# Zero products in fp32 instead of fp16, and two FFN blocks in two column pieces each

## The chip, the core and the metric

The kernel runs on one core of a Trainium2 chip. The metric is the time of one execution on the device in microseconds; the number for a kernel is the median of several runs. Profiled executions come with a span, from the first to the last instruction of the program, which is a little shorter than the device time of the same execution. TensorE (PE) multiplies, its weight loads (PEld) overlap with the products; VectorE (DVE), ScalarE (ACT) and GpSimd (POOL) do elementwise work; SyncE (SP) issues most of the transfers.

## The reference

A retention layer with a decaying state, step by step over 768 positions, for 4 batches and 8 heads of 64, then a feed-forward part with a product of two branches and no nonlinearity. All inputs and the output are fp32.

```python
gamma = 1.0 - 2.0 ** (-5.0 - np.arange(H))
for t in range(S):
    state = gamma * state + k[:, :, t] (x) v[:, :, t]       # 64 x 64 per head
    y[:, :, t] = q[:, :, t] @ state / sqrt(D)
x = y as 3072 rows of 512
out = ((x @ w1) * (x @ w2)) @ w3 @ w_out                    # 512 -> 1024 -> 512
```

## The kernel before

The 3072 rows are cut into twelve tiles of T = 256 positions, three to a batch, n = 0 to 11; the tile that the words call the seventh has n = 6. The recurrence is computed in chunks. For each tile there are `scores` (k against q inside a chunk, line 406), `kv` (the chunk's own state, line 454), `inter` (the carried state against q, line 521, in two halves with `fence` between them) and `av` (masked scores against v, line 548). All of these are 64x64 products that use one quarter of the array each; `QUARTERS` (line 377) names the four quarters in the order in which every group of four goes through them. The text calls them the quarter groups. `x_out` scales the result into `XT`, in fp16.

The feed-forward part multiplies w3 and w_out with each other first (`turn_w3`, `turned_w3`, `w3_mm`, `w3_out`; lines 278 to 307), as soon as their rows arrive, and keeps the product in `W3O`. Then each tile needs four pairs of blocks: `two_blocks` (line 578) makes 2 x 128 columns of x @ w1 ("a") or x @ w2 ("b") from eight products of 256 columns in one bank of PSUM; `a_evac` copies "a" out on ScalarE, `b_evac` multiplies it by "b" on VectorE. `blk` (line 704) calls `two_blocks`, and `evac` the two evacuations. `o_unit` (line 636) multiplies the result with `W3O`; it already has a parameter `pieces`, which the calls for n = 5 set to 2.

The order of everything is written out by hand, from line 713 to the end: each engine runs its own instructions in that order, with semaphores between engines. In the steady part one round is: the quarter groups of two neighbouring tiles, `o_unit` and `o_copy` of an earlier tile, then the eight blocks of a tile with their evacuations. The loads are issued by `fetch` and `load` on SyncE.

At the start TensorE has little to do, since the weights are still arriving. `warm(m, tag, w)` (line 688) then issues m products of zeros into a bank of PSUM that nobody reads: 128 x 128 zeros against w columns of zeros, from the tile `zeros` (line 135), which is 512 columns of fp16 and is cleared as 256 columns of fp32. Each call takes the bank `tag` anew. `warm(8)` stands ahead of the first transposes of w3 (`turn_w3(4, "S0")`), the calls with "F2" between the transposes of rows 4, 1 and 2.

Of the kernel before, what the change touches and what calls it, by code (L numbers as in the profile page):

```python
# [9 lines left out]
FP = mybir.dt.float32  # L10
# [10 lines left out]
def kernel(  # L21
# [11 lines left out]
    nc = tc.nc  # L33
    B, H, S, D = q.shape
    T = 256
# [35 lines left out]
    def bank(tag, shape, dtype=FP):  # L71
        return psum.tile(shape, dtype, tag=tag, name="ps" + tag)
# [47 lines left out]
    def fetch(names, via=nc.sync):  # L120
        for x in names.split():
            kind, i = x[:-1], int(x[-1])
            if kind == "r":
                w3_st[i] = load_rows(moe_w3, i, via)
            elif kind == "wo":
                wo_st[i] = load_wo(i, via)
            elif kind in ("w1", "w2"):
                w_st[kind, i] = load_rows({"w1": moe_w1, "w2": moe_w2}[kind], i, via)
            else:
                load(kind, i)  # L130
# [4 lines left out]
    zeros = const.tile([128, 512], HP, name="zeros")  # L135
# [14 lines left out]
    def need(*x):  # L150
        assert done.issuperset(x)

    def numbers():
        done.add("numbers")

        nc.gpsimd.iota(key_i[:, :, :], pattern=[[1, 2], [0, H]], base=1 - 128, channel_multiplier=2)
        nc.gpsimd.iota(
            col_i[:, :, :].rearrange("p g (j u) -> p g j u", j=8), pattern=[[128, 2], [1, 8], [8, 16]],
            base=1 - 128, channel_multiplier=0,
        )  # L160
        for h in range(H):
            p = h // 2
            c = place(p, h % 2) * 64
            nc.gpsimd.memset(LGH[:, h : h + 1], -math.log(gam[h]))
            nc.gpsimd.memset(LGP[c : c + 64, p : p + 1], math.log(gam[h]))

    def keeps():
        done.add("keeps")
        nc.gpsimd.memset(keep[:, :, :], 1.0)
        for g in range(2):  # L170
            rows = slice(g * 64, g * 64 + 64)
            for t in range(2):
                nc.gpsimd.affine_select(
                    out=keep[rows, t, :], in_=keep[rows, t, :], compare_op=GE, fill=0.0,
                    base=-t, pattern=[[1, 8], [8, 16]], channel_multiplier=-2,
                )
# [28 lines left out]
    W1 = [wpool.tile([128, DFF], HP, name=f"w1_{i}") for i in range(4)]  # L205
    W2 = [wpool.tile([128, DFF], HP, name=f"w2_{i}") for i in range(4)]
# [35 lines left out]
    def step_decays():  # L242
        done.add("decays")
        for h in range(H):
            r, p = (h % 2) * 64, h // 2
            nc.gpsimd.memset(GS[r : r + 64, p, :], gam[h] ** T)
# [22 lines left out]
    def cast_wo(i, eng):  # L269
        done.add(("wo", i))  # L270
        split(eng, WO[i][:, :, :].rearrange("p a n -> p (a n)"), wo_st[i][:, :])

    def cast_w3(f, eng):
        w3h[f] = att.tile([128, 1024], HP, tag="kq"[len(w3h_tags) % 2] + "16", name="w3h", bufs=3)
        w3h_tags.append(f)
        split(eng, w3h[f][:, :], w3_st[f][:, :])

    def turn_w3(f, tag):
        need("identity")
        src, ps = w3h.pop(f), bank(tag, [128, 1024], HP)  # L280
        for g in range(8):
            c0 = g // 2 * 256 + g % 2
            nc.tensor.transpose(ps[:, g * 128 : (g + 1) * 128], src[:, c0 : c0 + 255 : 2], ident16[:, :])  # L283
        w3p[f] = ps

    def turned_w3(f, eng):
        w3t[f] = fsb.tile([128, 1024], HP, tag="pa", name="w3t", bufs=8)
        split(eng, w3t[f][:, :], w3p.pop(f)[:, :])
# [23 lines left out]
    q16, k16, v16, qT, kT, qP, am, XT, TS, KB, X = {}, {}, {}, {}, {}, {}, {}, {}, {}, {}, {}  # L312
# [262 lines left out]

    HT, pa, ht_n = {}, {}, {}

    def two_blocks(W, n, u, tag):
        need(*[(w, d, c) for w in ("w1", "w2") for d in range(4) for c in (0, 512)])
        assert x_n[n] == 2  # L580
        ps = bank(tag, [128, 2, T])
        for i in range(2):
            f = 2 * u + i
            for d in range(4):
                nc.tensor.matmul(  # L585
                    ps[:, i, :], lhsT=W[d][:, f * 128 : (f + 1) * 128], rhs=XT[n][:, d, :],
                    start=(i == 0 and d == 0), stop=(i == 1 and d == 3),
                )
        return ps

    def a_evac(n, u, ps, eng="s"):
# [9 lines left out]
    def a_unit(n, u, tag, eng="s"):  # L601
        a_evac(n, u, two_blocks(W1, n, u, tag), eng)

    def b_unit(n, u, tag):
        b_evac(n, u, two_blocks(W2, n, u, tag))
# [54 lines left out]
    def o_copy(n, tb, c0=0, c1=512, eng="s"):  # L660
        dst, src = o_tile(n, tb)[:, c0:c1], o_ps.pop((n, tb, c0, c1))[:, :]
        if eng == "s":
            nc.scalar.activation(dst, src, AF.Copy, scale=final_scale)  # L663
        else:
            nc.vector.tensor_scalar_mul(dst, src, final_scale)
        o_n[n] = o_n.get(n, 0) + (c1 - c0)
        o_n[n, tb] = o_n.get((n, tb), 0) + (c1 - c0)
# [17 lines left out]
            o_copy(n, tb, *c)  # L685
            o_store(n, tb, *c)

    def warm(m, tag="X1", w=512):
        ps = bank(tag, [128, 512])
        for _ in range(m):  # L690
            nc.tensor.matmul(ps[:, 0:w], lhsT=zeros[:, 0:128], rhs=zeros[:, 0:w], start=True, stop=True)

    def cast_w(W, st, d, eng, c0=0, c1=DFF):
        done.update((st, d, c) for c in range(c0, c1, 512))
# [6 lines left out]
    ab = {}  # L701
    cuts = ((0, 320), (320, 512))

    def blk(w, n, u, tag):
        ab[w, n, u] = two_blocks(W1 if w == "a" else W2, n, u, tag)

    def evac(w, n, u, eng="s"):
        if w == "a":
            a_evac(n, u, ab.pop((w, n, u)), eng)
        else:  # L710
            b_evac(n, u, ab.pop((w, n, u)))
# [33 lines left out]
    fetch("q3")  # L745
    identity()
    fetch("q4")
    warm(8)
    numbers()
    arguments()  # L750
    tables(4)
# [2 lines left out]
    tables(2)  # L754
    cast_w3(4, "v")
    turn_w3(4, "S0")
    warm(3, "F2")
    turned_w3(4, "v")
    step_decays()
    warm(2, "F2")  # L760
    cast_wo(0, "s")
    cast_w3(1, "v")
    keeps()
    warm(1, "F2")
    cast_w3(2, "gs")
    warm(1, "F2")
    turn_w3(1, "S1")
    tables(0)
    fetch("v3")
    turned_w3(1, "sv")  # L770
    warm(3, "F2")
    cast_wo(1, "g")
    turn_w3(2, "X0")
    w3_mm(1, 0, "S1", first=True)
# [206 lines left out]
    x_out(2, 1)  # L981
    dma_turn("q", 4)
    blk("a", 2, 0, "F0")
    cast_v(4, "g")
    evac("a", 2, 0)
    blk("b", 2, 0, "F1")
    kv(3, ("X0", "K"))
    turned("q", 3, "v")
    state(3, 1)
    fetch("k5")  # L990
    fetch("v5")
    blk("b", 2, 1, "F0")
    state(3, 2)
    blk("a", 2, 1, "F2")
# [180 lines left out]
    o_copy(5, 0)  # L1175
    o_unit(5, 1, ("F0",), pieces=2)
    o_copy(5, 1)
    blk("a", 6, 0, "F2")
    evac("a", 6, 0)
    blk("b", 6, 0, "F0")  # L1180
    evac("b", 6, 0)
    blk("a", 6, 1, "F1")
    evac("a", 6, 1)
# [245 lines left out]
```

## Time and profile before

| | us |
|---|---|
| median of 3 runs | 181.31 |
| lowest and highest run | 181.07, 181.83 |
| the profiled execution, device time | 181.6 |
| its span | 179.9 |
| ScalarE, VectorE, GpSimd busy | 66.1, 103.0, 63.6 |

How to read it. A row of a timeline has the start and the time that the row covers in us, then engine, line, operation, output and inputs, shape, and the number of instructions that were merged into it; in square brackets stands idle time of the engine before it and what ended it. A matmul's duration in a row goes from its start to the end of its way through the array, and the next one starts well before that, so the rate of a row of products is seen from start to start: the time that the row covers, less one duration, over the number of products less one. In a row of a table by stretches come the stretch, its length, then busy us and number of instructions of PE, PEld, DVE, ACT and POOL, TensorE's granted clock, the busy share of the DMA engines and GB/s. In the chain of waits a line gives start, length and what the end waited for through that time; "SPq" is SyncE's queue. A group of the list of costly lines gives busy us in all and mean ns of one behind the first bar, idle time before it behind the second. A view of one tile or line gives the least, median and largest duration in ns and the first and last start. The row of an instruction queue (q8) gives packets, MB and the share of the DMA engines.

### The profile page before, as it was taken

To read this page: it belongs to the slowest core of one execution; us is meant where nothing else is said; L and a number is where in the kernel's file an instruction comes from. 1 tells how busy PE (TensorE), PEld (TensorE's weight loads), DVE (VectorE), ACT (ScalarE), POOL (GpSimd) and SP (SyncE) were. 2 spreads that over 40 slices of the span, in tenths; PEclk is the share of its full clock that TensorE was granted. 3 is DMA by queue.
4 is the path that set the end of the run, shared out by engine and by line. 5 is a ranking of instruction groups with operands and counts; after the bars stand their busy time and mean duration, and the time that the engine had idled before them with its cause. 6 is when DMAs were issued, how large, how long until landed. Compare 5 with 4: busy or idle time off the path is not lost.

```text
span 179.9 us, 6072 instructions
## 1 busy us (share of the span) xinstructions
PE 173.4 (96%) x2642; PEld 125.7 (70%) x2642; DVE 103.0 (57%) x177; ACT 66.1 (37%) x118; POOL 63.6 (35%) x93
## 2 busy tenths in 40 slices
PE   7989899999999999999999999999999999999993
PEld 2445456688956785885867898768688587786872
DVE  2342789883946487547366384474764946734330
ACT  5436537681238332323314314223222131232422
POOL 7753076446232742724445055250453200000000
PEclk9999999999999999999999999999999999999999
DMA  5999999999899899999999999999999552150303
GB/s 206 409 418 360 357 325 389 408 282 226 181 244 236 204 179 221 202 204 238 178 241 228 237 284 178 212 240 232 271 211 263 170 166 71 70 166 5 117 0 117
DMA packets 80025, 40.22 MB, mean 224 GB/s; under 512 B 59392, under 2 KB 73984, under 8 KB 80000
## 3 DMA queue, kind: packets, MB, share of 16 engines
q1 hardware_dynamic: 79856, 39.33, 88.6%
q8 instruction: 20, 0.33, 0.8%
q10 hardware_dynamic: 144, 0.52, 0.8%
q14 instruction: 5, 0.04, 0.1%
HBM read 29.36 MB, written 6.29 MB: 198 GB/s over the span
## 4 chain that ended last, share of the span: by engine, by line
PE 72%; DMA 15%; SPq 5%; POOL 3%; ACT 2%; DVE 1%; issue 1%; POOLq 0%; DVEq 0%
PE psF L585 38%; PE psF L643 20%; DMA st<-in_v_dram 8%; DMA st<-in_q_dram 4%; DMA st<-in_moe_w_dram 4%; SPq L112 3%; PE psX L521 2%; POOL v L69 2%; PE psX L548 2%; PE psS L406 1%; PE psK L299 1%; PE psF L299 1%; ACT pa L61 1%; SPq L89 1%; PE psF L621 1%; PE psX L621 1%
## 5 line engine op out<-in xcount | busy, mean ns | idle before, releaser
L585 PE MATMUL psF<-xt,w 128*128 128x256 f16 x640 | 71.9, 273 | 0.0
L585 PEld LDWEIGHTS <-w 128*128 128x128 f16 x640 | 62.4, 98 | 9.2
L69 DVE TENSOR_TENSOR ht<-pa,psF 128x512 f16<-128x512 f32 x43 | 29.4, 687 | 38.9 <-PE psF L585 38.8
L61 ACT COPY pa<-psF 128x512 f32<-128x512 f32 x43 | 25.2, 585 | 51.2 <-PE psF L585 45.6
L643 PE MATMUL psF<-w3o,ht 128*128 128x512 f16 (+3 forms) x200 | 38.4, 346 | 0.0
L643 PEld LDWEIGHTS <-ht 128*128 128x128 f16 x224 | 20.7, 98 | 17.5
L69 POOL TENSOR_TENSOR v<-st,VN 128x1024 f16<-128x1024 f32 x10 | 19.0, 1902 | 37.2 <-DMA st<-in_v_dram 18.5
L663 ACT ACTIVATE osb<-psF 128x512 f32<-128x512 f32 (+2 forms) x18 | 9.9, 550 | 31.0 <-PE psF L643 31.0
L566 DVE TENSOR_TENSOR xt<-psX,YN 128x512 f16<-128x512 f32 x19 | 12.8, 724 | 5.7 <-PE psX L548 5.7
L426 DVE TENSOR_TENSOR am<-psS,keep 128x512 f16<-128x512 f32 x19 | 12.5, 681 | 2.6 <-PE psF L406 2.6
L621 PEld LDWEIGHTS <-w 128*128 128x128 f16 x128 | 12.1, 98 | 2.4 <-issue 0.5
L61 POOL CAST q<-st 128x1024 f16<-128x1024 f32 x10 | 10.4, 1039 | 7.2 <-DMA st<-in_q_dram 4.3
L61 POOL CAST k<-st 128x1024 f16<-128x1024 f32 x9 | 9.3, 1036 | 6.2 <-PE psX L548 3.1
L299 PEld LDWEIGHTS <-w3t 128*128 128x128 f16 x64 | 5.8, 98 | 6.4 <-issue 0.7
L621 PE MATMUL psF<-xt,w 128*128 128x256 f16 x56 | 9.7, 272 | 0.0
L69 POOL TENSOR_TENSOR t<-s,GS 128x256 f16<-128x256 f32 x8 | 5.8, 727 | 11.0 <-DVE s L69 11.0
L521 PE MATMUL psX<-qT,t 64*64 64x64 f16 (+1 forms) x296 | 7.6, 199 | 0.0
L69 POOL TENSOR_TENSOR v<-st,VS 128x1024 f16<-128x1024 f32 x2 | 3.9, 1932 | 8.9 <-DMA st<-in_v_dram 8.9
L521 PEld LDWEIGHTS <-t 64*64 64x64 f16 x320 | 4.9, 106 | 3.0 <-issue 2.5
L69 DVE TENSOR_TENSOR t<-psK,t 128x256 f16<-128x256 f32 x15 | 6.2, 415 | 0.4
L283 PEld LDWEIGHTS <-w3h 128*128 128x128 f16 x64 | 4.2, 101 | 2.9 <-DVE w3h L61 1.4
L621 PE MATMUL psX<-xt,w 128*128 128x256 f16 x32 | 6.1, 273 | 0.1
(127 smaller groups left out, 192.4 us busy)
## 6 DMA issues: line engine op xcount, KB each, us to landing
st<-in_moe_w_dram SPq DMA_DIRECT2D x15, 512.0 KB, 8.7
st<-in_k_dram SPq DMA_DIRECT2D x20, 256.0 KB, 5.7
st<-in_q_dram SPq DMA_DIRECT2D x10, 512.0 KB, 6.1
st<-in_v_dram SPq DMA_DIRECT2D x20, 256.0 KB, 4.6
out_dram<-osb SPq DMA_DIRECT2D x9, 512.0 KB, 5.4
st<-in_moe_w_out_dram SPq DMA_DIRECT2D x4, 512.0 KB, 9.8
st<-in_k_dram SPq DMA_DIRECT2D x2, 512.0 KB, 6.5
st<-in_q_dram SPq DMA_DIRECT2D x8, 128.0 KB, 6.5
```

Of the source, the lines that this page charges most:

```text
L61: {"v": nc.vector.tensor_copy, "g": nc.gpsimd.tensor_copy, "s": nc.scalar.copy}[eng](dst, src)
L69: (nc.vector if eng == "v" else nc.gpsimd).tensor_tensor(dst, a, b, op)
L112: via.dma_start(t[:, :].rearrange("p (t n) -> p t n", t=2), moe_w_out[i * 256 : (i + 1) * 256, :].rearrange("(p t) n -> p t n", t=2),)
L283: nc.tensor.transpose(ps[:, g * 128 : (g + 1) * 128], src[:, c0 : c0 + 255 : 2], ident16[:, :])
L299: nc.tensor.matmul(acc[f][:, :], lhsT=w3t[f][:, g * 128 : (g + 1) * 128], rhs=WO[i][:, r, :], start=(first and r == 0), stop=(last and r = ...
L426: nc.vector.tensor_tensor(t[:, :, :, :].rearrange("p a s i -> p (a s) i"), ps[:, :, :, :].rearrange("p a s i -> p (a s) i"), keep64[:, :]. ...
L521: nc.tensor.matmul(dst, lhsT=TS[n, c][half(r), a, :], rhs=rhs, start=((g, o) not in begun), stop=False, skip_group_check=True,)
L566: nc.vector.tensor_tensor(XT[n][:, :, :].rearrange("p a (s x) -> p (a s) x", s=2)[:, :, g * 64 : (g + 1) * 64].rearrange("p k (i t) -> p k ...
L585: nc.tensor.matmul(ps[:, i, :], lhsT=W[d][:, f * 128 : (f + 1) * 128], rhs=XT[n][:, d, :], start=(i == 0 and d == 0), stop=(i == 1 and d = ...
L621: nc.tensor.matmul(rows_ps[w, n, uh][j // 2][:, j % 2, :], lhsT=W[d][:, f * 128 : (f + 1) * 128], rhs=XT[n][:, d, :], start=(first and j % ...
L643: nc.tensor.matmul(ps[:, x : x + w], lhsT=HT[n][:, f, tb * 128 : (tb + 1) * 128], rhs=W3O[f][:, c0 + x : c0 + x + w], start=(f == 0 and x ...
L663: nc.scalar.activation(dst, src, AF.Copy, scale=final_scale)
```

## The change

`warm` reads the zeros as fp32: the same memory as 256 columns instead of 512, the weights as 128 x 128 of fp32. Its default is now 256 columns, and the calls are written anew: four products for the first eight, then 256 columns for each two and 128 for each odd one of the rest. A call has one width, so an odd number takes two calls. That makes eleven zero products instead of eighteen. `two_blocks` and `blk` get a parameter `pieces`; with 2, each product of 256 columns is made as two of 128 with the same weights, each with a load of its own. The first two blocks of n = 6 are called so: 32 products instead of 16. What is computed stays the same.

```diff
--- before.py
+++ after.py
@@ -575,17 +575,19 @@
 
     HT, pa, ht_n = {}, {}, {}
 
-    def two_blocks(W, n, u, tag):
+    def two_blocks(W, n, u, tag, pieces=1):
         need(*[(w, d, c) for w in ("w1", "w2") for d in range(4) for c in (0, 512)])
         assert x_n[n] == 2
         ps = bank(tag, [128, 2, T])
         for i in range(2):
             f = 2 * u + i
             for d in range(4):
-                nc.tensor.matmul(
-                    ps[:, i, :], lhsT=W[d][:, f * 128 : (f + 1) * 128], rhs=XT[n][:, d, :],
-                    start=(i == 0 and d == 0), stop=(i == 1 and d == 3),
-                )
+                for x in range(0, T, T // pieces):
+                    nc.tensor.matmul(
+                        ps[:, i, x : x + T // pieces], lhsT=W[d][:, f * 128 : (f + 1) * 128],
+                        rhs=XT[n][:, d, x : x + T // pieces], start=(i == 0 and d == 0 and x == 0),
+                        stop=(i == 1 and d == 3), skip_group_check=pieces > 1,
+                    )
         return ps
 
     def a_evac(n, u, ps, eng="s"):
@@ -685,10 +687,10 @@
             o_copy(n, tb, *c)
             o_store(n, tb, *c)
 
-    def warm(m, tag="X1", w=512):
-        ps = bank(tag, [128, 512])
+    def warm(m, tag="X1", w=256):
+        ps, z = bank(tag, [128, 512]), zeros[:, :].bitcast(FP)
         for _ in range(m):
-            nc.tensor.matmul(ps[:, 0:w], lhsT=zeros[:, 0:128], rhs=zeros[:, 0:w], start=True, stop=True)
+            nc.tensor.matmul(ps[:, 0:w], lhsT=z[:, 0:128], rhs=z[:, 0:w], start=True, stop=True)
 
     def cast_w(W, st, d, eng, c0=0, c1=DFF):
         done.update((st, d, c) for c in range(c0, c1, 512))
@@ -701,8 +703,8 @@
     ab = {}
     cuts = ((0, 320), (320, 512))
 
-    def blk(w, n, u, tag):
-        ab[w, n, u] = two_blocks(W1 if w == "a" else W2, n, u, tag)
+    def blk(w, n, u, tag, pieces=1):
+        ab[w, n, u] = two_blocks(W1 if w == "a" else W2, n, u, tag, pieces)
 
     def evac(w, n, u, eng="s"):
         if w == "a":
@@ -745,7 +747,7 @@
     fetch("q3")
     identity()
     fetch("q4")
-    warm(8)
+    warm(4)
     numbers()
     arguments()
     tables(4)
@@ -754,21 +756,23 @@
     tables(2)
     cast_w3(4, "v")
     turn_w3(4, "S0")
-    warm(3, "F2")
+    warm(1, "F2")
+    warm(1, "F2", w=128)
     turned_w3(4, "v")
     step_decays()
-    warm(2, "F2")
+    warm(1, "F2")
     cast_wo(0, "s")
     cast_w3(1, "v")
     keeps()
-    warm(1, "F2")
+    warm(1, "F2", w=128)
     cast_w3(2, "gs")
-    warm(1, "F2")
+    warm(1, "F2", w=128)
     turn_w3(1, "S1")
     tables(0)
     fetch("v3")
     turned_w3(1, "sv")
-    warm(3, "F2")
+    warm(1, "F2")
+    warm(1, "F2", w=128)
     cast_wo(1, "g")
     turn_w3(2, "X0")
     w3_mm(1, 0, "S1", first=True)
@@ -1175,9 +1179,9 @@
     o_copy(5, 0)
     o_unit(5, 1, ("F0",), pieces=2)
     o_copy(5, 1)
-    blk("a", 6, 0, "F2")
+    blk("a", 6, 0, "F2", pieces=2)
     evac("a", 6, 0)
-    blk("b", 6, 0, "F0")
+    blk("b", 6, 0, "F0", pieces=2)
     evac("b", 6, 0)
     blk("a", 6, 1, "F1")
     evac("a", 6, 1)
```

## The prediction

> **What bounds the kernel now.** I read the page first: busy time by engine, then the chain that ended last, then the costliest groups.
>
> ```profile
> span 179.9 us, 6072 instructions
> PE 173.4 (96%) x2642; PEld 125.7 (70%) x2642; DVE 103.0 (57%) x177; ACT 66.1 (37%) x118; POOL 63.6 (35%) x93
> ...
> PE 72%; DMA 15%; SPq 5%; POOL 3%; ACT 2%; DVE 1%; issue 1%; POOLq 0%; DVEq 0%
> ```
>
> TensorE is busy for 96% of the span and holds 72% of the chain. The 15% of DMA is not spread evenly; the chain in order of time, between 8 and 24 us, and the timeline of the first 23 us show where TensorE has room.
>
> ```profile
> 8.18 4.31 SPq L112
> ...
> 14.66 7.06 DMA st<-in_q_dram
> ...
> 21.84 0.70 DVE q L61
> ...
> 22.59 0.62 PE psX L370 x8
> ```
>
> ```profile
> 1.26 3.59 PE L691 MATMUL psX<-zeros 128*128 128x512 f16 x8 [1.26 <-DVE zeros L136]
> ...
> 4.77 0.66 PEld L283 LDWEIGHTS <-w3h 128*128 128x128 f16 x8 [0.83 <-DVE w3h L61]
> ...
> 5.44 2.32 PE L691 MATMUL psF<-zeros 128*128 128x512 f16 x7
> ...
> 7.60 0.45 PEld L283 LDWEIGHTS <-w3h 128*128 128x128 f16 x8 [0.54 <-DVE w3h L61]
> 7.61 0.62 PE L283 MATMUL psS<-ident,w3h 128*128 128x128 f16 x8
> ...
> 8.06 0.81 PE L691 MATMUL psF<-zeros 128*128 128x512 f16 x3
> ...
> 8.95 0.45 PEld L283 LDWEIGHTS <-w3h 128*128 128x128 f16 x8 [0.58 <-POOL w3h L61]
> ...
> 9.12 0.56 ACT L61 COPY w3t<-psS 128x512 f16<-128x512 f16 x1
> ...
> 10.06 0.68 DVE L61 COPY w3t<-psX 128x1024 f16<-128x1024 f16 x1
> ...
> 10.20 1.02 PE L299 MATMUL psS<-wo,w3t 128*128 128x512 f16 x4 [0.62 <-DVE w3t L61]
> ...
> 13.15 0.59 PE L299 MATMUL psS<-wo,w3t 128*128 128x512 f16 x2 [0.19 <-POOL wo L61]
> ...
> 22.59 0.62 PE L370 MATMUL psX<-perm,q 128*128 128x128 f16 x8 [0.59 <-DVE q L61]
> ```
>
> The reader is to see two things. The zero products of line 691 all lie before 9 us, between transposes that wait for casts of weights still arriving. And until 22.59 us the chain runs through SyncE's queue and the landing of the first q; TensorE stands idle before 10.20, 13.15 and 22.59 us for 0.62 + 0.19 + 0.59 = 1.40 us. Later there is one more wait for a cast of v, of 0.33 us; from then to the last store TensorE is continuously busy, so what happens there counts in full.
>
> ```profile
> 61.60 0.19 PE L454 MATMUL psX<-v,k 64*64 64x64 f16 x1 [0.33 <-POOL v L69]
> ```
>
> The other place that the change touches is this steady part. Between two rows of FFN blocks lies a burst of 64x64 products, the quarter groups: some 120 products in 1.2 us. I compared the bursts of the seventh and the tenth tile (inter of n = 6 and n = 9), which issue the same products in the same order; first by stretches, then the end of each in the timeline.
>
> ```profile
> 103.00:104.17 1.17, 1.17 (x122) 1.13 (x121) 0.69 (x1) 0.15 (x1) 0.35 (x1) 1.00 1.22 217
> 138.23:139.57 1.34, 1.34 (x121) 1.26 (x120) 0.69 (x1) 0.15 (x1) 1.34 (x1) 1.00 0.92 180
> ...
> 114.75:115.91 1.16, 1.16 (x121) 1.12 (x120) 0.69 (x1) 0.15 (x1) 0.28 (x1) 1.00 1.11 221
> 150.12:151.28 1.16, 1.16 (x121) 1.12 (x121) 0.69 (x1) 0.15 (x1) 0.00 (x0) 1.00 0.02 7
> ```
>
> ```profile
> 102.80 0.27 PE L585 MATMUL psF<-xt,w 128*128 128x256 f16 x1
> 103.00 0.28 PE L521 MATMUL psX<-qT,t 64*64 64x64 f16 x10
> ...
> 103.68 0.29 PE L521 MATMUL psX<-qT,t 64*64 64x64 f16 x11
> ...
> 103.80 0.44 PE L548 MATMUL psX<-am,v 64*64 64x64 f16 x31
> 104.17 0.39 PE L643 MATMUL psF<-w3o,ht 128*128 128x256 f16 x2
> ```
>
> ```profile
> 138.91 0.41 PE L521 MATMUL psX<-qT,t 64*64 64x64 f16 x12
> 139.15 0.49 PE L548 MATMUL psX<-am,v 64*64 64x64 f16 x32
> 139.57 0.39 PE L643 MATMUL psF<-w3o,ht 128*128 128x512 f16 x1
> ```
>
> The tenth tile's burst is 0.17 us longer. 0.12 of it lies in the second half of inter (0.41 against 0.29) and 0.05 in av behind it, and no semaphore is named there. Other bursts repeat to 0.01 us (1.16 and 1.16 for n = 7 and n = 10).
>
> **The change part by part.**
>
> *Zero products, cold.* Eight of 512 columns become four of 256. In the old ones a start follows a start by (3.59 - 0.63) / 7 = 0.42 us with 0.63 the duration of one; the later ones by (0.81 - 0.38) / 2 = 0.216 us.
>
> ```profile
> L691 PE MATMUL psF<-zeros x10: 376/379/379, 5.4 to 8.5; 128*128 128x512 f16 x10
> L691 PE MATMUL psX<-zeros x8: 606/631/631, 1.3 to 4.2; 128*128 128x512 f16 x8
> ```
>
> No fp32 product is in this trace. From below, its 256 columns could take what 256 fp16 columns take, half of 0.42 us; from above I let it take twice the pair that it replaces, 1.7 us. I take the pair, 0.85 us, because the edit exchanges them two for one all through (512 for 256, and a single one for 128 columns), and the rows in between give no better price. Then the four end at 4.65 us as before, ahead of the cast that releases the transposes at 4.77. Were they shorter, TensorE would only idle until then; and should the spacing of 0.216 then come later than it does now, the next seven at 0.42 would add 1.5 us, which the cover of the next step and the 1.40 us of idle time hide.
> The Trainium skill ("FP8 and Floating Point Precision", section "TensorE Precision Notes") says "True FP32: 4 passes through PE array": 4 x 256 columns are the 1024 of the pair, so by it this term is nothing too; no run here shows it yet.
>
> *Zero products, later.* Seven behind the first transposes and three behind the second become two groups of the same worth, 7 and 3 halves of a fp32 product. But each call takes the bank anew and waits for the call before it. In the row of 5.44 us three such waits stand: 2.16 us to the next start at 7.60, less 7 x 0.216, is 0.65, or 0.215 each. The new list makes five calls instead of four behind the first transposes, and two instead of one behind the second: 0.215 us more each. So the transposes of 7.61 start at 7.82, those of 8.96 at 7.82 + 0.45 + 0.65 + 0.215 = 9.13. What covers it: ScalarE begins the first copy at 9.12, when those transposes (now done by 8.5) have long ended; VectorE begins the second at 10.06, and they end by 9.75. Cost 0. Without this cover it would be 0.43 us at 10.20, and behind that the 0.19 + 0.59 us of waits for POOL and for q still take it.
> A rule that speaks against the change: the Trainium skill ("TensorE: Matmul & The Clock Gate", section "Weight-path perf modes — Fast Weight Load (FWL) and DoubleRow") grants the fast weight load to types other than FP32 only. If each of four passes then waited for a load of 128 columns at the P / 1.2 of the same page (section "LDWEIGHTS (loading the stationary operand)"), 107 ns, a 128-column product would cost 0.43 us, an estimate from that page, and the four of them 0.85 us more; the idle times above would still hide that.
>
> *The two blocks in pieces.* 16 products of 256 columns become 32 of 128, each with its own weight load. They lie in the part that counts.
>
> ```profile
> L585 PE MATMUL psF<-xt,w 128*128 128x256 f16 x640 | 71.9, 273 | 0.0
> L585 PEld LDWEIGHTS <-w 128*128 128x128 f16 x640 | 62.4, 98 | 9.2
> ```
>
> ```profile
> L283 PE MATMUL psF<-ident,w3h x24: 219/219/219, 15.8 to 27.6; 128*128 128x128 f16 x24
> ```
>
> A 256-column product takes 71.9 / 640 = 0.112 us, which holds the starts of rows; inside a row it is nearer 0.109. The nearest row to the new form is the transposes at full speed, 128 columns with a 128-column load each: (0.62 - 0.22) / 7 = 0.057 us. Two of them are 0.114, so 16 x (0.114 - 0.109) = +0.08 us at most; I take +0.05. From below 0; from above, loads that no longer overlap, 32 x 0.098 = 3.1 us against 1.8, or +1.3 us, which the transposes speak against. The evacuations wait for the last product as before.
>
> *The positions.* Every instruction behind the start moves in TensorE's stream: eleven zero products instead of eighteen, then sixteen more from the seventh tile on. What a position is worth is not a row; its bounds are. From above, the stall of the tenth tile in every burst; from below, groups of four at the rate of their columns (64 of 256 columns, a quarter of 0.109 = 0.027 us per four) instead of 0.033 (1.16 us less two changes of shape of 0.09 each, as 103.00 - 102.80 less 0.109 shows one, over 30 groups): 0.17 us for each of 8 bursts. I take the row: eight of nine bursts run without a stall, so the one that has it most likely loses it when it is moved, -0.17 us, and the others keep what they have.
>
> Sum: 0 + 0 + 0.05 - 0.17 = -0.12 us. Against the profiled execution's 181.6 us (span 179.9 and 1.7 around it) that is 181.5; the median of the runs is 181.31, so 181.2.
>
> **The rivals.**
>
> *Stalls in many bursts (slower).* Eight bursts that now run clean meet at their new place what the tenth tile's meets now. For it: the same products cost 0.17 us more at one place than at another, with nothing waited for, and the stream's instructions come in pieces:
>
> ```profile
> q8 instruction: 20, 0.33, 0.8%
> ```
>
> 20 packets for 5284 TensorE instructions are one per 264, or 132 products, about the length of a burst, so a burst that lies badly against them meets the border every time. Against it: nearly every burst crosses a border now, and only one is longer. Price 8 x 0.17 = 1.4, and 0.05: 182.7 us. It decides from six bursts up (+0.9 us).
>
> *fp32 products cost more than the pair (slower).* At twice the pair the first four end 3.4 us later, of which 0.1 is the wait at 4.77; the seven halves add 1.5. The transposes of 7.61 come at 12.4; 1.06 us of that lies free before ScalarE's copy at 9.12, then 0.19 and 0.59 follow: about 2.9 us late at 22.59, less the 0.33 at 61.60: 183.9 us. From 1.5 times the pair it shows. Against it: nothing but the two-for-one exchange.
>
> *All groups run better (faster).* 8 x 0.17 from the lower bound of the positions, and the stall: with what the pieces cost, 180.0 at the extreme, 180.2 if most of it comes. Against it: the equal bursts have had different places already and agree to 0.01 us.
>
> *The position does nothing.* The stall belongs to the tenth tile wherever it stands, or merely moves: 181.31 + 0.05 = 181.4 us.
>
> **How the numbers follow.** The forecast 0.52, its own range 180.9 to 181.7; no effect of position 0.15; stalls in many bursts 0.18; dearer fp32 0.06; all groups better 0.09. A measurement of this kernel tells about 0.5%, 0.9 us, from no change. So faster is 0.09, slower 0.18 + 0.06 = 0.24, within 0.67. The range reaches up to the stalls, 182.6, and down to 180.5, half of the way to better groups; it leaves out the dearer fp32 and the extremes.
>
> **What would show it.** Right: 22.59 us still begins with TensorE idle for q; transposes near 4.8, 7.8 and 9.1 us; the pieces' blocks 0.03 us longer each at most; the burst of n = 9 at 1.17 us and the others as now. Wrong: TensorE busy without a gap up to q's transposes (dear fp32 products), bursts of 1.3 us and more in several tiles (stalls), or bursts near 1.0 us (better groups). A row of FFN blocks that begins or ends later than its products need would mean a mechanism that none of this has.

## The result and the profile after

The changed kernel takes 183.26 us (median of 22 runs, 180.99 to 184.37) against 181.18 us (22 runs, 180.76 to 182.64). The ratio is 1.0073, 95% interval 1.0052 to 1.0094: slower, by more than the 0.5% that counts as a difference here. The ratio leaves out runs more than 1.5% above the fastest of their kernel, six of the changed kernel's and none of before, and the profiled execution (184.05 us, at a granted clock of 1.00) is one of the six. The medians of all runs lie 1.1% apart.

The page of the changed kernel: engines, chain, and the row of the instruction queue.

```profile
span 182.2 us, 6112 instructions
...
PE 174.5 (96%) x2662; PEld 128.3 (70%) x2662; DVE 103.0 (57%) x177; ACT 66.1 (36%) x118; POOL 64.1 (35%) x93
...
q8 instruction: 20, 0.33, 0.9%
...
PE 82%; DMA 7%; SPq 4%; DVE 3%; issue 2%; ACT 0%; DVEq 0%
```

TensorE has 2662 products where 2642 stood, 20 more, and not the nine more that the number of written products (18 to 11, and 16 more) would give. The view of the tile of zeros tells why.

```profile
L693 PEld LDWEIGHTS psF<-zeros x14: 186/189/192, 5.4 to 9.6; 128*128 128x128 f32 x14
L693 PE MATMUL psF<-zeros x14: 275/377/483, 5.5 to 9.7; 128*128 128x128 f32 x8, 128*128 128x256 f32 x6
...
L693 PE MATMUL psX<-zeros x8: 531/634/795, 1.3 to 4.4; 128*128 128x256 f32 x8
```

Eleven fp32 products are 22 loads and 22 products on the engine. So everything behind them moves by 22 - 18 = 4 products, and by 20 from the seventh tile on. The timeline of TensorE, and then that of its loads, shows where the time is lost: TensorE stands still in three places, at the bursts of n = 5, n = 8 and n = 10.

```profile
92.07 1.47 PE L645 MATMUL psF<-w3o,ht 128*128 128x512 f16 x6
93.75 1.45 PE L645 MATMUL psF<-w3o,ht 128*128 128x512 f16 x6 [0.21 <-DVE xt L566]
...
127.70 1.47 PE L645 MATMUL psF<-w3o,ht 128*128 128x512 f16 x6
129.98 1.24 PE L645 MATMUL psF<-w3o,ht 128*128 128x512 f16 x5 [0.81 <-DVE t L69]
...
151.87 0.38 PE L548 MATMUL psX<-am,v 64*64 64x64 f16 x22
153.40 0.28 PE L548 MATMUL psX<-am,v 64*64 64x64 f16 x10 [1.15 <-issue]
```

```profile
129.99 0.96 PEld L645 LDWEIGHTS <-ht 128*128 128x128 f16 x5 [1.09 <-issue]
...
153.40 0.17 PEld L548 LDWEIGHTS <-v 64*64 64x64 f16 x9 [1.26 <-issue]
```

Six products of `o_unit`, then nothing, then the rest of the same `o_unit`; and in the third, 22 products of av, nothing for more than a microsecond, then the last ten. In the kernel before, the same av and `o_unit` of n = 10 run through:

```profile
150.88 0.46 PE L548 MATMUL psX<-am,v 64*64 64x64 f16 x32
151.28 3.63 PE L643 MATMUL psF<-w3o,ht 128*128 128x512 f16 x16
```

VectorE is named in two of the rows, but neither of the tiles named (`xt`, `t`) is an input of the product behind the gap, which is the seventh of eight that add up in one bank; and the loads' row says "issue", that is, nothing that the profile shows. From start to start, less the usual distance, the three gaps are 0.37, 0.97 and 1.34 us, 2.68 together. The span grew by 2.3; the burst of n = 4's kv starts at 61.17 instead of 61.60, since its cast of v was not waited for, and that gives 0.43 back.

If TensorE's products are numbered from 0 in the order of their starts, the first products behind the gaps are 1372, 2012 and 2396. Their distances are 640 and 384: five times and three times 128. With a load each, 128 products are 256 instructions, and 20 packets of the queue cover 5324 instructions, one per 266.

### The profile page after: what moved, and what is told of

Its sections match the earlier page's. It is cut to its first block, busy times and chain, and to the rows that moved or that the text cites. A ratio compares the mean times of both kernels' runs of the same rounds, so it can differ in the third digit from the quotient of the medians.

```text
span 182.2 us, 6112 instructions
## 1 busy us (share of the span) xinstructions
PE 174.5 (96%) x2662; PEld 128.3 (70%) x2662; DVE 103.0 (57%) x177; ACT 66.1 (36%) x118; POOL 64.1 (35%) x93
## 4 chain that ended last, share of the span: by engine, by line
PE 82%; DMA 7%; SPq 4%; DVE 3%; issue 2%; ACT 0%; DVEq 0%
PE psF L586 38%; PE psF L645 19%; DMA st<-in_q_dram 4%; DMA st<-in_moe_w_dram 3%; PE psF L623 3%; SPq L112 3%; PE psX L521 2%; PE psX L548 2%; PE psX L623 2%; PE psX L645 2%; PE psS L406 2%; PE psS L623 2%; PE psK L299 1%; PE psF L299 1%; SPq L89 1%
## 5 line engine op out<-in xcount | busy, mean ns | idle before, releaser
L586 PE MATMUL psF<-xt,w 128*128 128x256 f16 (+1 forms) x656 | 71.9, 270 | 0.0
L623 PE MATMUL psF<-xt,w 128*128 128x256 f16 x56 | 9.7, 272 | 0.0
L548 PE MATMUL psX<-am,v 64*64 64x64 f16 (+1 forms) x336 | 6.2, 197 | 1.2 <-issue 1.2
```

Source lines behind the costliest of these rows:

```text
L548: nc.tensor.matmul(o, lhsT=v16[n][half(g), t, h * D : (h + 1) * D], rhs=rhs, start=((g, c) not in begun), stop=(n >= EO or t == 1), skip_g ...
L586: nc.tensor.matmul(ps[:, i, x : x + T // pieces], lhsT=W[d][:, f * 128 : (f + 1) * 128], rhs=XT[n][:, d, x : x + T // pieces], start=(i == ...
L623: nc.tensor.matmul(rows_ps[w, n, uh][j // 2][:, j % 2, :], lhsT=W[d][:, f * 128 : (f + 1) * 128], rhs=XT[n][:, d, :], start=(first and j % ...
```

## The experiments

The theory after the result, P: TensorE's instructions arrive in blocks of 128 products (with the loads, 256 instructions), with borders at products 92, 220, ... 1244, 1372, ..., counted in steps of 128 from the gaps. A burst eats 120 to 128 products in 1.2 us. If one border lies at its start, the next lies at its end, and its block has not yet arrived. Rivals: F, the fp32 products themselves; C, the pieces themselves.

**The zero products alone.** The changed kernel without the pieces.

```diff
-    blk("a", 6, 0, "F2", pieces=2)
+    blk("a", 6, 0, "F2")
-    blk("b", 6, 0, "F0", pieces=2)
+    blk("b", 6, 0, "F0")
```

> The zero products of the change alone, without the pieces. Theory P (place in TensorE's instruction stream: a burst of quarter groups uses up a block of 256 instructions, 128 products, before the next one has arrived): eleven fp32 products leave 22 records where eighteen stood, so everything behind moves by 4. The ends of blocks then fall on products 1372 (n = 5, in o_unit right behind the burst, as in the changed kernel) and 2396 (n = 10, 126 products behind the burst's start, so in o_unit and not inside av); the one that stood behind the burst of n = 8 is now 16 products later and harmless. Idle TensorE of 0.2 to 1.3 us in n = 5 and n = 10, none in n = 8; time 181.5 to 183. Rival F (fp32 products themselves cost): as the changed kernel, about 183.2, with the time lost before 23 us. Rival C (the pieces cost): as before, 181.2.

181.96 us (12 runs), ratio 1.0021, 95% interval 0.9994 to 1.0047: not told from no change. The profiled execution (182.82 us) has its gaps at products 1372 (0.59 us) and 2396 (1.18 us), both expected, and none in n = 8.

**The pieces alone.** The zero products of before, and the two blocks of n = 6 in pieces.

> The two blocks in pieces, with the zero products of before. Theory P: nothing moves up to the seventh tile, then 16 products. n = 5 stays as in the kernel before (its border 138 products behind the burst's start, no stall seen). n = 8 gets a border at the same 138: none or little. n = 10 gets one 114 products behind the burst's start, inside av: a stall of 0.5 to 1.5 us there. Time 181.5 to 182.7. Rival F: 181.2 as before, no stall. Rival C (the pieces themselves): about 183, and the rows of the two blocks longer than 0.9 us each.

181.91 us, ratio 1.0027, 0.9997 to 1.0058, again not told from no change. The one gap of the profiled execution is at product 2012, behind the burst of n = 8, 0.49 us, where little or none was expected; and n = 10, where it was expected, has none. The place was on the list of borders, the choice among them was wrong: the two borders in n = 10 are nearer in time, but the packet with its block began earlier (the table below).

**The same places in fp16.** Zero products in fp16, with four more of them, and the pieces. The cut shows what differs from the kernel before, without the pieces.

```diff
     keeps()
-    warm(1, "F2")
+    warm(2, "F2", w=256)
...
     turned_w3(1, "sv")
-    warm(3, "F2")
+    warm(6, "F2", w=256)
```

> fp16 zero products as before, but four of 512 columns in two of 256 columns each, so that four more products stand in the stream, and the pieces: every instruction of the steady part has the place that it has in the changed kernel, without one fp32 product. Theory P: stalls at the same products (1372, 2012, 2396), time as the changed kernel, 182 to 184. Rival F: as with the pieces alone.

183.70 us, ratio 1.0066, 1.0030 to 1.0102: the loss of the changed kernel without an fp32 product in it. F falls. Of the three gaps that were expected, its profiled execution (182.17 us) has one of 0.34 us at 1372 and none at 2012 and 2396; one of 0.15 us lies at 1628, a border that falls into the pieces. So with the same places not the same borders stall in two executions, and the time varies as well, 181.19 to 184.81.

**The fp32 products at the places of before.** Nine instead of eleven, no pieces. One zero product of 128 columns is left out. The cut shows what differs from the changed kernel, without the pieces.

```diff
     warm(1, "F2")
-    warm(1, "F2", w=128)
     turned_w3(4, "v")
...
     keeps()
-    warm(1, "F2", w=128)
+    warm(1, "F2")
     cast_w3(2, "gs")
...
     turned_w3(1, "sv")
     warm(1, "F2")
-    warm(1, "F2", w=128)
```

> fp32 zero products, but nine of them, 18 records as the eighteen of before, and no pieces: the steady part stands where it stood before the change. It leaves out one zero product of 128 columns and three calls; nothing of what is computed. Theory P: as before, 181.2 within 0.3, no stall but perhaps the one of 0.1 us in n = 9. Rival F: slower than before by 1 us or more.

181.26 us, ratio 0.9980, 0.9955 to 1.0004, and no gap at a border. With the run before this settles that the places cost, and not fp32.

**Bad places.** The theory was then asked for a kernel slower than the changed one: the fp16 zero products of before with the same columns of zeros in ten more products, and the pieces, so that the bursts of n = 5 and n = 8 fill a block from border to border. The cut shows the zero products against the kernel before.

```diff
-    warm(3, "F2")
+    warm(6, "F2", w=256)
-    warm(2, "F2")
+    warm(4, "F2", w=256)
-    warm(1, "F2")
+    warm(2, "F2", w=256)
-    warm(1, "F2")
+    warm(2, "F2", w=256)
-    warm(3, "F2")
+    warm(6, "F2", w=256)
```

> fp16 throughout: the ten later zero products of 512 columns each become two of 256 (the same columns of zeros, ten more products), and the two blocks stay in pieces. Theory P: everything behind moves by 10, and by 26 from the seventh tile on, so that the bursts of n = 5 and n = 8 begin exactly at a border and end at the next one: by the trace of before the two borders are 1.23 us apart in both. With 2.7 us and more from the request to the first instruction of a new block, TensorE stands 1.3 to 2.5 us at product 1372 and at product 2012, and little or nothing in n = 10. Time 184 to 186.5, worse than the changed kernel. A rival that holds fp32 or the pieces to blame, or the number of calls, expects about 181.9 as with the pieces alone.

186.31 us (6 runs, 183.49 to 188.49); the ratio, which rests on two of the six, is 1.0162, 1.0104 to 1.0221. The kernel with the same pieces at other places (the pieces alone) took 181.91, so C falls too. The timeline of TensorE behind the bursts of n = 5 and n = 8:

```profile
91.56 0.48 PE L548 MATMUL psX<-am,v 64*64 64x64 f16 x32
93.96 1.24 PE L645 MATMUL psF<-w3o,ht 128*128 128x512 f16 x5 [1.93 <-issue]
```

```profile
129.46 0.62 PE L548 MATMUL psX<-am,v 64*64 64x64 f16 x32
131.33 1.02 PE L645 MATMUL psF<-w3o,ht 128*128 128x512 f16 x4 [1.25 <-issue]
```

Now the gap stands exactly between the last product of the burst and the first of `o_unit`, which is product 1372 and 2012, and "issue" is named. There is a third of 1.28 us at 2396 in n = 10, where little or nothing was expected: its borders are 3.6 us apart, but the packet started late. A fourth, of 0.47 us, lies at 1628 in the pieces.

**Good places.** The kernel before, with five of the ten later zero products left out.

```diff
-    warm(3, "F2")
+    warm(2, "F2")
-    warm(2, "F2")
+    warm(1, "F2")
     keeps()
-    warm(1, "F2")
...
     turned_w3(1, "sv")
-    warm(3, "F2")
+    warm(1, "F2")
```

> fp16, no pieces, five of the ten later zero products left out (nothing of what is computed): everything behind moves by 5 the other way. Theory P: no two borders that follow each other are closer than 3.7 us in the steady part, so no burst waits for instructions; as before or faster by up to 0.3 us, 180.9 to 181.3, and a smaller spread than before. A rival in which zero products keep the clock up expects more than 181.3.

181.21 us, ratio 1.0003, 0.9980 to 1.0027. No gap at any border; but no gain, and no smaller spread. The burst of n = 9 has a wait of 0.95 us instead, and its row names it:

```profile
138.36 0.45 PE L406 MATMUL psS<-qT,kT 64*64 64x64 f16 x32 [0.78 <-DMA qT<-q]
```

TensorE begins this burst 1.1 us sooner than in the profile of before (137.15 against 138.23) and now waits for q's transposes of n = 10. SyncE's queue in the same run:

```profile
125.88 1.31 SPq L94 DMA_DIRECT2D st<-in_q_dram  x1
127.29 2.50 SPq L679 DMA_DIRECT2D out_dram<-osb  x1
129.88 1.76 SPq L357 DMA_TRANSPOSE kT<-k  x1
131.75 2.27 SPq L357 DMA_TRANSPOSE qT<-q  x1
```

The store of the output of n = 5 holds the queue for 2.50 us ahead of the two transposes.

**Good places, and that store behind the transposes; and the same store moved with nine fp32 products.** In both, in SyncE's queue:

```diff
     load("q", 11)
-    o_store_all(5)
...
     dma_turn("q", 10)
+    o_store_all(5)
```

> The kernel of the good places (five zero products fewer), with one edit on SyncE's queue: the store of the output of n = 5 is issued behind the two transposes of n = 10 instead of ahead of them. Theory P says that in the good places the 0.97 us before scores of n = 10 (in the burst of n = 9) is the next bound: q's transposes land late because 2.5 us of that store stand ahead of them on the queue. Then the wait goes or shrinks below 0.3 us and the time is 180.3 to 181.0, faster than before. If the transposes wait for something else, the wait stays and the time is 181.2.

> Nine fp32 zero products at the places of before (one of 128 columns left out), with the same edit on SyncE's queue. Theory P: its wait of 0.29 us before the same scores goes; 180.9 to 181.3. In the places of before the border of n = 10 is still near, so it gains less than the kernel of the good places.

The first takes 180.56 us, ratio 0.9941, 0.9919 to 0.9964: faster than the kernel before and than the changed one. Eleven of its 12 runs lie between 180.39 and 181.18, the twelfth is 184.62. SyncE's queue and the burst of n = 9 in it:

```profile
126.37 3.83 SPq L357 DMA_TRANSPOSE kT<-k  x1
130.31 1.42 SPq L357 DMA_TRANSPOSE qT<-q  x1
131.82 0.53 SPq L679 DMA_DIRECT2D out_dram<-osb  x1
```

```profile
137.49 0.28 PE L521 MATMUL psX<-qT,t 64*64 64x64 f16 x10
...
138.67 1.69 PE L643 MATMUL psF<-w3o,ht 128*128 128x512 f16 x7
```

The queue issues k's transpose at 126.37 instead of 129.88 us and q's at 130.31 instead of 131.75, and the burst takes 1.18 us with no wait. The second takes 181.17 us, 0.9979, 0.9951 to 1.0007; its wait (0.28 us with nine fp32 products) is gone as well, but a gain is not told from none. So one edit alone gave nothing that could be measured, twice, and both together 0.6%: in the kernel of the good places the transposes are the next bound.

That the borders of the steady part are what the two kernels with the later store differ by is not shown. From the burst of n = 3 to the end both profiled executions take 111.92 us, without a gap at a border; the 0.26 us between their spans lie ahead of it. There the last part of the first q lands at 20.29 and 20.27 us in the two kernels with five zero products left out, whose first instruction packet begins at 20.3 us, and between 21.6 and 21.8 us in the seven other traces that record its landing, whose packet begins between 18.7 and 19.5. Whether that packet holds up q's load is not shown; no run moves the one without the other.

**Borders and gaps in one table.** Every gap at a border of more than 0.1 us in the steady part, and some borders without one. Worked out from the traces: the start of the product at the first border, the start of the queue's packet that belongs to the block behind the next border, and the product at that next border. "Apart" is the time between the two products less the gap; "packet" is counted from the first product.

| kernel, burst | borders, products into the burst | apart, us | packet, us | gap, us | packet to next border, us |
|---|---|---|---|---|---|
| before, n = 5 | 10, 138 | 3.3 | +0.6 | 0 | 2.7 |
| before, n = 10 | 2, 130 | 3.3 | -0.8 | 0 | 4.1 |
| changed, n = 5 | 6, 134 | 2.5 | +0.1 | 0.37 | 2.7 |
| changed, n = 8 | 6, 134 | 2.5 | +0.7 | 0.97 | 2.7 |
| changed, n = 10 | -18, 110 | 3.0 | +1.9 | 1.34 | 2.4 |
| fp32 alone, n = 5 | 6, 134 | 2.5 | +0.4 | 0.59 | 2.7 |
| fp32 alone, n = 10 | -2, 126 | 2.8 | +1.6 | 1.18 | 2.4 |
| pieces alone, n = 8 | 10, 138 | 3.3 | +1.2 | 0.49 | 2.6 |
| pieces alone, n = 10 | -14, 114 | 2.6 | -1.0 | 0 | 3.6 |
| fp16 same places, n = 5 | 6, 134 | 2.5 | -0.1 | 0.34 | 2.9 |
| fp16 same places, n = 8 | 6, 134 | 2.5 | -0.5 | 0 | 3.0 |
| bad places, n = 5 | 0, 128 | 1.2 | +0.3 | 2.0 | 2.9 |
| bad places, n = 8 | 0, 128 | 1.4 | +0.2 | 1.3 | 2.5 |
| bad places, n = 10 | -24, 104 | 3.6 | +2.6 | 1.28 | 2.2 |
| bad places, pieces after n = 6 | 48, 176 | 5.6 | +3.6 | 0.47 | 2.5 |
| fp16 same places, pieces after n = 6 | 54, 182 | 5.9 | +3.7 | 0.15 | 2.3 |

The last column is the evidence: wherever TensorE stood, its next product came 2.2 to 2.9 us after the packet began, and no border in the table that came more than 2.9 us after its packet has a gap. The same holds for all 194 borders that can be paired with a packet in the ten traces. None comes less than 2.24 us after its packet; 17 come within 2.91 us, the twelve of the table and five without such a gap (n = 5 of before is one), and no later one has a gap. The packet itself begins, in the table, between 1.0 us ahead of the first border and 3.7 us behind it. That could be what spreads the runs, which is not shown; what sets the start of the packet was not tried.

The Trainium skill ("Runtime: NRT & Kernel Launch", section "Instruction fetch mechanics") tells of blocks of 256 instructions that are fetched while the one before runs. The traces agree with the size: 128 products with a load each from border to border, and packets of 0.33 MB / 20, some 16 KB. The same section of the Trainium skill calls the cost of a border mostly hidden; here it was up to 2.0 us at one border.

## Why the prediction was wrong

*What bounds the kernel* held: the start is bound by transfers, the steady part by TensorE, and a loss in a burst counts in full.

*Zero products, cold and later:* cost 0, right. For the first four the price held: behind the first one the records follow each other every 0.427 us, two to a product, which is 0.85 us for the pair's 0.85; only the first took 0.18 us longer. The transposes start at 4.99 instead of 4.77 us, but for another reason: the cast that they wait for ends at 4.93 instead of 4.71.

```profile
4.24 0.69 DVE L61 CAST w3h<-st 128x1024 f16<-128x1024 f32 x1 [0.40 <-DMA st<-in_moe_w_dram]
4.99 0.45 PEld L283 LDWEIGHTS <-w3h 128*128 128x128 f16 x8 [0.68 <-DVE w3h L61]
```

For the later ones the price was too low: the transposes forecast at 7.82 and 9.13 came at 8.33 and 9.81. All of it was hidden, as the row of q's transposes shows in the changed kernel, at the same time as before:

```profile
22.59 0.62 PE L370 MATMUL psX<-perm,q 128*128 128x128 f16 x8 [0.67 <-DVE q L61]
```

Among these later ones a 256-column product took an estimated 0.49 us (0.71 from one call to the next, less the wait of 0.215) instead of the 0.43 of its pair, and a 128-column one 0.33 us (0.55 less 0.215) instead of 0.22. The load of fp32 weights took 189 ns there against 98 in fp16. The rule of the Trainium skill ("TensorE: Matmul & The Clock Gate", section "Weight-path perf modes — Fast Weight Load (FWL) and DoubleRow") that the fast weight load is not for fp32 agrees with that. The trace has two loads to a product, not four, and the 0.43 us that the prediction estimated for 128 columns by that rule did not come.

*The two blocks in pieces:* right. 32 products of 128 columns took 1.79 us from start to start, 16 of 256 take 1.75: +0.04.

*The positions:* the step that failed. It said that "eight of nine bursts run without a stall, so the one that has it most likely loses it when it is moved, -0.17 us, and the others keep what they have". Three things in it were wrong. The stall of the tenth tile was taken for the price of a place; it is not. Moved by 20 products, the burst did not come down to the forecast 1.17 us but took its 1.34 us again:

```profile
139.22:140.56 1.34, 1.34 (x121) 1.26 (x121) 0.69 (x1) 0.15 (x1) 0.28 (x1) 1.00 1.13 349
```

In this and five further profiles gaps of 0.03 to 0.95 us stand in that burst, at products 2192, 2129, 2110 and 2165, 2158, 2094 and 2089 where it was 2153 (the run with the bad places has small ones in n = 7 and n = 8 instead), so it goes with the tile and not with the place. The gaps at the last two products are waits for the transposes, and there is none in the two profiles with the store moved. Secondly the shift was counted as eleven products for eighteen, 7 to the front, when it was 4 to the back. And the price of a border was bounded by that stall, 0.17 us, when a late block costs what it is late, up to 1.34 us in the changed kernel. In the kernel before, the bursts of n = 5 and n = 10 were clean because their borders happened to be 3.3 us apart and their packets began early enough (2.7 and 4.1 us ahead of the next border).

*The rivals.* "Stalls in many bursts" had the carrier right, the packet per 132 products and the border that a burst crosses, and the sign. It did not reach the condition. Not the crossing of one border costs, as "nearly every burst crosses a border now" rightly held against it, but a next border that comes before its block is there, because the two lie close in time or because the packet began late. So three bursts paid up to 1.34 us each instead of eight that pay 0.17; that its 182.7 us lies near the 183.26 measured is luck. Dearer fp32 products are out, since q's transposes still start at 22.59 us, and so are better groups, since the bursts without a gap still take 1.16 to 1.23 us. Two counts in this part are off: the trace has eight such bursts in all (n = 3 to 10), so seven and not eight ran clean, and the terms of the better groups, with the stall, add up to 179.8 and not 180.0 us. Neither changes the forecast.

The range ended at 182.6 us, below the median of 183.26.

## What to carry to other kernels

Where a stretch of many short products runs through a few hundred instructions in a microsecond, count the instructions from one such stretch to the next: an edit ahead of it that adds or removes TensorE instructions, even for work that nobody waits for, moves the borders of the instruction blocks, and a kernel that was measured good may stand just beside a bad place. Idle time whose next instruction has no reason to wait, at distances that are multiples of one number of instructions, is the sign. Once a gap has shown where the borders lie, the trace of before holds the times from border to border, and from them the good and bad shifts can be reckoned. The reckoning is rough, since the start of the packet varies: it was right for the bad and the good places and wrong for n = 8 and n = 10 with the pieces alone. Once that is out of the way look at the next wait: here a store ahead of two transposes on one queue.

## What the runs showed of the hardware

The profile puts a gap at a border down to an engine on which the product does not depend (VectorE in two of the three of the changed kernel) or to "issue"; the row of the loads is the better witness. An fp32 product is two records, each with its own load, and two speeds stand in the trace: in the first four products, where 512 fp16 columns took 0.43 us before, a load takes 337 ns and the 256 columns 0.85 us, as much as the two fp16 products that they replace; in the later ones, where 512 fp16 columns took 0.22 us, a load takes 189 ns and the 256 columns an estimated 0.49 us against 0.43. Two things stay open: what sets the start of an instruction packet, and what makes the gaps in the burst of n = 9 that name no semaphore. These gaps were gone in the two profiles with the store moved, which suggests the transfers and does not show it.
